# Two more token pairs transposed by way of DRAM, the key sum read as a row of G, and statistics and normalisation moved to ScalarE

## The chip, the core and the metric

The kernel runs on one core of a Trainium2 chip. The metric is the device time of one execution in microseconds (us). Five engines work side by side, each through its own queue in order: PE (TensorE, matrix products), DVE (VectorE), ACT (ScalarE), POOL (GpSimd) and SP (SyncE, which only issues transfers here). They wait for each other on semaphores. L12 is line 12 of the kernel.

## The reference, cut to what matters

Inputs are x of 2048 tokens by 512, weights wqkv (512 x 1536) and wo (512 x 512), and w_gate, w_up (512 x 1792) and w_down (1792 x 512).

```python
xn = (x - mean) / sqrt(var + 1e-5)                 # over the 512 columns
q, k, v = heads of xn @ wqkv                       # 32 heads of 16
phi(t) = where(t > 0, t + 1, exp(t)) + 1e-6
kv  = einsum("bhsd,bhse->bhde", phi(k), v)
z   = einsum("bhsd->bhd", phi(k))
num = einsum("bhqd,bhde->bhqe", phi(q), kv)
den = einsum("bhqd,bhd->bhq", phi(q), z)[..., None] + 1e-6
s   = (num / den) @ wo
g   = silu((gelu(xn @ w_gate) * (xn @ w_up)) @ w_down)
out = x + s * g
```

## The kernel before, in words

The 2048 tokens are 16 tiles of 128 rows. Two tiles make a pair, and there are 8 pairs (n = 0 to 7): pair 0 is tiles 0 and 4, pair 1 is 1 and 5, pair 2 is 2 and 6, pair 3 is 3 and 7, pairs 4 to 7 are (8, 12), (9, 13), (10, 14), (11, 15). Every float32 operand of a large product is split in a high and a low part (`split`: ACT makes the high part, DVE or POOL the low one), and a product is three passes of PE: high by high, high by low, low by high. Most large products are done by a scheme of 7 block products in place of 8 (X, Y and Z are its PSUM banks in the attention part; FX, FY, FZ and dX, dY, dZ in the feed-forward part).

The stages are these. First come the tokens, up to some 125 us: `ln` normalises a tile (statistics by two DVE instructions, the inverse root by POOL, xn by DVE), `transp` turns it, `split_x` and `forms` make the operands of the products, and q and k follow, with `phi` on ACT and DVE. `gacc` accumulates G = xn^T phi(k) in four banks (gps). Then kv = Wv^T G (pkv, L988) and M = kv wo (pm) are made once. Then the feed-forward part runs for the second half of the tokens (p = 1) and the first half (p = 0); between them the accumulators of p = 1 go through silu on ACT. Last come s = phi(q)/den M (sps) and the output.

Names that the change touches:

- `transp` (L621): for pairs below TX, PE turns the four 128 x 128 blocks of a tile (pt, L643) and ACT copies the bank. From TX on, xn is made by ACT (L565), written to DRAM (xn_d), read back in another layout (xq), and turned by one DVE instruction (`squares`, L617). TX is 6, so pairs 6 and 7 go by DRAM.
- `phi` (L705): for each tile two ACT instructions (relu of -v, exp) and one DVE instruction.
- `zacc` (L722): POOL adds phi(k) of each tile to an accumulator; at the end two PE passes (pz, L933) sum it over rows, and ACT copies it to zq. POOL multiplies phi(q) by zq for the denominators (L960).
- ACT holds one table of functions at a time: one for exp, one for gelu, one for silu. Each change issues an ACT_TABLE_LOAD.
- `warm` (L472): 12 products of a constant with itself ahead of the first real work on PE.

The order on every engine is not that of the code. The code makes a list of some 3,600 operations with their dependencies, and `ORDER` (L18) is a written-out permutation of that list: operation numbers in the order in which they are issued, each to its engine's queue. So each engine's queue is a subsequence of ORDER.

Of the kernel before, what the change touches and what calls it, by code (L numbers as in the profile page):

```python
# [14 lines left out]
P = 128  # L15
# [147 lines left out]
]  # L163

TABLES = {"exp": "exp", "gelu": "gelu", "silu": "silu"}
# [123 lines left out]
def pool(n):  # L289
    return 0.18 + 0.0021 * n  # L290
# [1168 lines left out]
```

## Time and profile before

| | |
|---|---|
| three runs | 566.92, 567.49, 567.54 us; median 567.49 |
| the profiled execution | 566.9 us in all, of which the span from first to last instruction is 564.8 us |
| PE busy | 557.8 us, 2630 matmul records |
| DVE busy | 493.2 us |
| ACT busy | 360.8 us |
| POOL busy | 253.1 us |
| transfers | 141.29 MB, mean 250 GB/s |

The time of the profiled execution lies 2.1 us above its span (566.9 less 564.8). "Busy" of PE counts pipelined products whose ends are modelled, so the distance between two starts tells more than a duration. In rows of the timeline the first column is the start in us from the span's start, the second how long the row's instructions took together, and the bracket at the end says how long the engine was idle ahead of it and what ended that.

### The profile page before, as it was taken

What the parts mean: (1) busy time and instruction counts of PE and PEld (TensorE: products, weight loads), DVE (VectorE), ACT (ScalarE), POOL (GpSimd) and SP (SyncE); (2) the same over time, 40 slices, a digit from 0 to 9 for tenths busy, and PEclk for the clock granted to TensorE, in tenths of its full rate; (3) what the DMA queues carried; (4) which work ended last, traced back from release to release, by engine and by line L of the source; (5) the groups of instructions that cost most, each with busy time, mean ns of one, the idle gap of its engine ahead of it and who ended that gap; (6) DMA issues with size and microseconds to landing.
All of it is one profiled execution on the core that took longest, in us unless ns stands there. A gap on an engine that the chain in (4) does not pass through costs nothing.

```text
span 564.8 us, 7902 instructions
## 1 busy us (share of the span) xinstructions
PE 557.8 (99%) x2630; PEld 487.0 (86%) x2630; DVE 493.2 (87%) x774; ACT 360.8 (64%) x668; POOL 253.1 (45%) x237
## 2 busy tenths in 40 slices
PE   8999999999999999999999999999999999999997
PEld 6888888888888888888888888888888888888886
DVE  7999999987798999999888776774889989898997
ACT  5987898877677876564536467867555636354730
POOL 4656677757786876431251940430413212314200
PEclk9999999999999999999999999999999999999999
DMA  7378967879978668158867998696757475778776
GB/s 266 104 217 273 274 203 233 255 223 322 352 241 300 240 234 339 43 201 311 265 233 216 389 339 335 239 344 254 243 187 242 173 247 194 233 228 286 239 247 239
DMA packets 78952, 141.29 MB, mean 250 GB/s; under 512 B 4672, under 2 KB 47680, under 8 KB 74944
## 3 DMA queue, kind: packets, MB, share of 16 engines
q1 hardware_dynamic: 78912, 140.79, 72.9%
q8 instruction: 21, 0.34, 0.2%
q14 instruction: 19, 0.16, 0.1%
HBM read 87.82 MB, written 52.95 MB: 249 GB/s over the span
## 4 chain that ended last, share of the span: by engine, by line
PE 91%; DVE 5%; DMA 2%; issue 1%; SPq 1%; ACT 0%; DVEq 0%; ACTq 0%
PE FX L442 26%; PE FZ L442 13%; PE dX L442 12%; PE gps L442 7%; PE FY L442 6%; PE dY L442 6%; PE X L442 6%; PE sps L442 4%; PE dZ L442 3%; PE Z L442 3%; PE q L442 2%; PE k L442 2%; PE Y L442 1%; DVE acc L1119 1%; PE pt L643 1%; DMA wk<-in_A_wqkv 1%
## 5 line engine op out<-in xcount | busy, mean ns | idle before, releaser
L442 PE MATMUL FX<-Xh,w 128*128 128x512 f32 x448 | 125.4, 379 | 0.0
L442 PEld LDWEIGHTS FX<-Xh,w 128*128 128x128 f32 x448 | 84.7, 189 | 12.0
L404 POOL TENSOR_TENSOR sums<-draw 128x256 f32<-128x256 f32 x28 | 26.5, 951 | 109.6 <-DVE dl L404 56.3
L1165 POOL TENSOR_TENSOR h<-h,g 128x512 f32<-128x512 f32 x28 | 39.5, 1411 | 65.9 <-DVE h L404 64.2
L442 PE MATMUL FX<-Xl,w 128*128 128x512 f32 x224 | 66.0, 379 | 0.0
L442 PE MATMUL FZ<-Xh,w 128*128 128x512 f32 x224 | 64.4, 379 | 0.0
L398 ACT COPY dY<-dX 128x512 f32<-128x512 f32 x56 | 32.1, 573 | 46.2 <-DVE acc L1119 28.4
L398 ACT COPY fu<-FX 128x512 f32<-128x512 f32 x56 | 32.7, 585 | 23.3 <-PE FX L442 19.4
L442 PEld LDWEIGHTS FX<-Xl,w 128*128 128x128 f32 x224 | 42.3, 189 | 6.0
L442 PEld LDWEIGHTS FZ<-Xh,w 128*128 128x128 f32 x224 | 42.3, 189 | 6.0
L398 ACT CAST hfh<-sums 128x512 fp32r<-128x512 f32 x56 | 34.5, 619 | 14.3 <-DVE sums L404 14.3
L442 PE MATMUL dX<-hfh,dh 128*128 128x512 f32 x112 | 41.9, 380 | 0.1
L442 PE MATMUL dX<-hfl,dh 128*128 128x512 f32 x112 | 41.5, 380 | 0.0
L442 PE MATMUL dX<-hfh,dl 128*128 128x512 f32 x112 | 41.0, 379 | 0.0
L1119 DVE TENSOR_TENSOR acc<-acc,dY 128x512 f32<-128x512 f32 x48 | 32.7, 681 | 8.9 <-PE dY L442 8.7
L404 DVE TENSOR_TENSOR hfl<-sums,hfh 128x512 fp32r<-128x512 f32 x56 | 40.2, 728 | 0.1
L404 POOL TENSOR_TENSOR tmp<-raw 128x256 f32<-128x256 f32 x28 | 29.1, 1049 | 20.1 <-DVE we L404 10.6
L1119 DVE TENSOR_TENSOR acc<-acc,dX 128x512 f32<-128x512 f32 x48 | 32.7, 683 | 5.5 <-PE dX L442 5.2
L960 POOL TENSOR_TENSOR qz<-qz,zq 128x512 f32<-128x512 f32 x16 | 23.3, 1456 | 23.1 <-DMA qz<-q_d 18.3
L442 PE MATMUL FY<-Xh,w 128*128 128x512 f32 x112 | 33.1, 379 | 0.0
L442 PE MATMUL FZ<-Xl,w 128*128 128x512 f32 x112 | 33.0, 379 | 0.0
L404 DVE TENSOR_TENSOR hfl<-h,hfh 128x512 fp32r<-128x512 f32 x42 | 32.2, 774 | 0.6 <-ACT hfh L398 0.6
(222 smaller groups left out, 1517.7 us busy)
## 6 DMA issues: line engine op xcount, KB each, us to landing
w<-w_d SPq DMA_DIRECT2D x17, 1792.0 KB, 7.9
w_d<-w SPq DMA_DIRECT2D x11, 1792.0 KB, 8.8
draw<-in_B_w_down SPq DMA_DIRECT2D x14, 512.0 KB, 4.0
w_d<-we SPq DMA_DIRECT2D x18, 256.0 KB, 2.2
x<-in_A_x SPq DMA_DIRECT2D x16, 256.0 KB, 3.3
q_d<-qp SPq DMA_DIRECT2D x16, 256.0 KB, 3.7
qz<-q_d SPq DMA_DIRECT2D x16, 256.0 KB, 3.1
q<-q_d SPq DMA_DIRECT2D x16, 256.0 KB, 3.8
```

What stands on the lines that cost most here:

```text
L398: do("ACT", act(n, src.psum), lambda o, i: nc.scalar.copy(o, i), dst, src, name=name)
L404: do(eng, c, lambda o, p, q: getattr(e, f"tensor_{op}")(o, p, q), dst, a, b, name=name)
L442: nc.tensor.matmul(o if r is None else o[:, r], a, turned(b), start=first, stop=made == self.passes[r], skip_group_check=self.on or r is n ...
L643: nc.tensor.transpose(o[:, k, :], a[:, j * P:(j + 1) * P], b)
L960: do("POOL", pool(D), lambda o, z: nc.gpsimd.tensor_mul(o, o, z.unsqueeze(1).to_broadcast([P, KT, P])), rows_of(q), zq, name="u")
L1119: do("DVE", dve(D), lambda o, i: nc.vector.tensor_add(o, o, i), o, ps, name="acc")
L1165: do("POOL", pool(NC), lambda o, i: nc.gpsimd.tensor_mul(o, o, i), h, g, name="h")
```

## The change

ORDER is written anew from end to end (3,622 operations), so all engines' queues differ. The code changes beside it are:

- TX goes from 6 to 4: pairs 4 and 5 go by DRAM too, and PE turns 8 tiles in place of 12.
- For tiles 2, 6, 3 and 7 (`XA`) xn is made by ACT, with a small DVE instruction for the bias (nb).
- For tile 4 (`SUMMED`), the second tile that is used, mean and variance come from two ACT instructions with an accumulated output (a copy and a square); DVE's two statistics instructions of it go.
- `added` adds 1 as well, so that `phi` on its results needs one ACT instruction (exp with a bias of -1) in place of two; this holds for 12 of the 32 calls.
- zacc and its 16 POOL additions, the two PE passes and the copies to zq go. In their place column 0 of each xn tile is set to 1 (16 small DVE instructions) ahead of its split, so that row 0 of G is the sum of phi(k). That row goes to DRAM and comes back spread over the partitions by four transfers. Because a row of xn sums to zero, subtracting the first row of Wv from all its rows makes up for the lost column (four subtractions, two by POOL and two by DVE).
- The warm-up products are 16 in place of 12.

```diff
 ORDER = [
-    988, 5, 0, 4, 7, 2, 10, 8, 11, 12, 9, 17, 6, 1, 18, 24, 16, 19, 20, 15, 28, 25, 13, 21, 29, 56, 62, 61, 63, 65, 116, 14, 57, 75, 117, 58, 118, 67,
...
-WARM = 12, 2
+WARM = 16,2
...
+    z_d = dram_view([1, D], "z_d")
...
-    zacc = const("zacc", [P, D])
-    do("POOL", 0.6, lambda o: nc.gpsimd.memset(o, NT * EPS), zacc)
...
-    TX = 6
+    TX = 4
...
+    XA = [(2, 6), (3, 7)]
+
+    SUMMED = [(4,)]
...
+        if ts in SUMMED:
...
+                for k, f in enumerate((AF.Copy, AF.Square)):
+                    do("ACT", 0.75, lambda o, a, x, b=None, f=f: nc.scalar.activation(o, x, f, accum_out=a, **({} if b is None else {"bias": b})),
+                       xns[t], mv[:, i, k:k + 1], xs[t], *([mv[:, i, 0:1]] if k else []), more=(mv,), name="sum")
...
+        if ts in XA:
+            nb = little("nb", f"nb{ts[0]}", [P, n])
...
+                do("ACT", 0.72, lambda o, i, r, b: nc.scalar.activation(o, i, AF.Identity, bias=b, scale=r),
+                   v, xs.pop(t).map(lambda ap: ap.rearrange("p (q g d) -> p q g d", q=KT, d=32)), rstd[:, i:i + 1], nb[:, i:i + 1], name=f"xn{t}")
...
+        do("DVE", 0.1, lambda o: nc.vector.memset(o, 1.0), (x[0] if isinstance(x, tuple) else x)[:, 0:1], name="one", port=False)
...
-        tt("DVE", "add", c, e, ps, D, name)
+        do("DVE", 0.6, lambda o, i, j: nc.vector.scalar_tensor_tensor(o, i, 1.0, j, op0=ALU.add, op1=ALU.add), c, ps, e, name=name)
...
+        if not v.psum:
+            do("ACT", act(D), lambda o, i, b: nc.scalar.activation(o, i, AF.Exp, bias=b), r, v, neg_one, name="exp")
+            p0 = U("p", range(24, 28), f"{nm}p{t}")
+            do("DVE", 0.6, lambda o, i, j: nc.vector.scalar_tensor_tensor(o, i, 1.0, j, op0=ALU.min, op1=ALU.max),
+               p0, r, v, name="phi")
+            return p0
...
-        do("POOL", pool(D), lambda o, i: nc.gpsimd.tensor_add(o, o, i), zacc, p0, name="zacc")
...
-    do("PE", 2 * PASS, run_z, pz, ones_r, *zs, key="z")
...
+    dma(z_d(0, slice(None)), GT[0][0:1], 2)
+    for k in range(KT):
+        dma(zq[32 * k:32 * k + 32].map(lambda ap: ap.rearrange("p (g d) -> p g d", d=32)),
+            z_d(0, slice(None)).map(lambda ap, k=k: ap.rearrange("o (g q d) -> o q g d", q=KT, d=32)[:, k].to_broadcast([32, KT, 32])), 16)
...
+    w0 = tile_in("up", 29, [P, D], F32, "w0")
+    dma(w0, ext(wqkv[0:1, 2 * D:3 * D].to_broadcast([P, D])), 256)
+    for c in range(KT):
+        tt("DVE" if c % 2 else "POOL", "sub", wv[c], wv[c], w0, D, "wv")
```

What the new ORDER makes of the queues is shown at three places. In the rows, x4 and xn4 are tile 4 and its normalised form, pt4 its bank of transposes, kq the split weights of q and k, k00 the first product bank (tile 0), Xh and Xl the split operands.

The first place is the start. PE's queue before:

```order
L472 MATMUL warm_100<-blk_93 128x128 x12
L643 MATMUL pt0_154<-blk_93,xn0_148 128x128 x4
L472 MATMUL warm_100<-blk_93 128x128 x2
L442 MATMUL k00_170<-kq0_135,Xh0_163 128x512
L442 MATMUL k00_170<-kq1_150,Xh0_163 128x512
L442 MATMUL k00_170<-kq0_135,Xh0_163 128x512 x3
L643 MATMUL pt4_196<-blk_93,xn4_189 128x128 x4
```

PE's queue there now:

```order
L473 MATMUL warm_101<-blk_94 128x128 x16
L680 MATMUL pt0_165<-blk_94,xn0_158 128x128 x2
L473 MATMUL warm_101<-blk_94 128x128 x2
L680 MATMUL pt0_165<-blk_94,xn0_158 128x128 x2
L443 MATMUL k00_193<-kq0_138,Xh0_182 128x512 x2
L680 MATMUL pt4_199<-blk_94,xn4_150 128x128 x4
```

Two products of k00 stand ahead of tile 4's transposes where five stood. DVE's queue at the same place before, from the variance of tile 0 on:

```order
L555 TENSOR_SCALAR ve0_139<-mv0_133 128x1
L573 TENSOR_SCALAR xn0_148<-x0_97,mv0_133,rstd0_141 128x4x4x32
L552 BN_STATS st4_152<-x4_121 128x6
L552 BN_STATS st1_165<-x1_123 128x6
L553 BN_AGGR mv4_168<-st4_152 128x2
L553 BN_AGGR mv1_172<-st1_165 128x2
L555 TENSOR_SCALAR ve4_174<-mv4_168 128x1
L552 BN_STATS st5_176<-x5_125 128x6
L553 BN_AGGR mv1_172<-st5_176 128x2
L555 TENSOR_SCALAR ve1_186<-mv1_172 128x2
L573 TENSOR_SCALAR xn4_189<-x4_121,mv4_168,rstd4_179 128x4x4x32
```

DVE's queue there now:

```order
L581 TENSOR_SCALAR ve0_144<-mv0_136 128x1
L566 TENSOR_SCALAR mv4_151<-mv4_151 128x1
L610 TENSOR_SCALAR xn0_158<-x0_98,mv0_136,rstd0_146 128x4x4x32
L578 BN_STATS st1_163<-x1_128 128x6
L563 TENSOR_SCALAR ve4_172<-mv4_151 128x1
L579 BN_AGGR mv1_174<-st1_163 128x2
L578 BN_STATS st5_176<-x5_130 128x6
L579 BN_AGGR mv1_174<-st5_176 128x2
L724 MEMSET xn0_158 128x1
L581 TENSOR_SCALAR ve1_187<-mv1_174 128x2
L571 TENSOR_SCALAR xn4_150<-x4_124,mv4_151,rstd4_180 128x4x4x32
```

A small instruction on tile 4's sum (L566) now stands ahead of xn0, and xn4 still stands behind the statistics of tiles 1 and 5. In SP's queue the load of x4 has moved from fourth to third place, ahead of the second piece of weights.

The second place is the switch between the two halves of the feed-forward part, on ACT. (FY, fu and dY are copies out of PSUM, g is gelu, acc1 under L1346 or L1380 is silu on the finished accumulators.) A piece of ACT's queue there before:

```order
L1079 ACT_TABLE_LOAD
L1079 ACTIVATE g22_14_3783<-g22_14_3783 128x512
L398 CAST hfh0_0_3826<-h11_15_3820 128x512
L1079 ACTIVATE g21_14_3831<-FX14_3612 128x512
L1346 ACT_TABLE_LOAD
L1346 ACTIVATE acc1_0_2134<-acc1_0_2134 128x512
L398 COPY fu3_15_3852<-FX15_3698 128x512
L1346 ACTIVATE acc1_1_2261<-acc1_1_2261 128x512
```

The tightest piece of it now:

```order
L399 COPY FY18_4078<-FX18_4054 128x512
L399 COPY dY00_0_4004<-dX00_0_3908 128x512
L1380 ACT_TABLE_LOAD
L1380 ACTIVATE acc1_1_2305<-acc1_1_2305 128x512
L1113 ACT_TABLE_LOAD
L1113 ACTIVATE g12_16_4032<-g12_16_4032 128x512
L399 COPY acc0_2_4119<-dY00_0_4004 128x512
L399 COPY fu2_18_4126<-FX18_4054 128x512
```

The silus are spread more thinly among the gelus: ACT's whole queue held 7 table loads before and holds 11 now, and all four new ones are at this switch (8 there in place of 4).

The third place is the end. The last rows of PE before (sps131 and sps130 are the two halves of the last tile, 256 columns each):

```order
L442 MATMUL sps130_5812<-pqh_5417,Ml_5157 128x256 x4
L442 MATMUL sps131_5800<-pqh_5417,Mh0_4075 128x256 x2
L442 MATMUL sps131_5800<-pqh_5417,Mh1_4270 128x256 x2
L442 MATMUL sps131_5800<-pqh_5417,Mh0_4075 128x256 x2
L442 MATMUL sps131_5800<-pqh_5417,Mh1_4270 128x256 x2
L442 MATMUL sps130_5812<-pqh_5417,Mh0_4075 128x256 x2
L442 MATMUL sps130_5812<-pqh_5417,Mh1_4270 128x256 x2
L442 MATMUL sps130_5812<-pqh_5417,Mh0_4075 128x256 x2
L442 MATMUL sps130_5812<-pqh_5417,Mh1_4270 128x256 x2
```

The last rows of PE now:

```order
L443 MATMUL sps131_5785<-pqh_5456,Ml_5152 128x256 x4
L443 MATMUL sps131_5785<-pqh_5456,Mh0_4406 128x256 x2
L443 MATMUL sps131_5785<-pqh_5456,Mh1_4330 128x256 x2
L443 MATMUL sps10_5808<-pqh_5456,Ml_5152 128x512 x4
L443 MATMUL sps10_5808<-pqh_5456,Mh0_4406 128x512 x2
L443 MATMUL sps10_5808<-pqh_5456,Mh1_4330 128x512 x2
L443 MATMUL sps10_5808<-pqh_5456,Mh0_4406 128x512 x2
L443 MATMUL sps10_5808<-pqh_5456,Mh1_4330 128x512 x2
```

The halves come earlier, and the last thing that PE makes is a whole tile of 512 columns (sps10); DVE's last two instructions and the last transfer have its size.

More of the change, by code (lines that the diff above doesn't have):

```diff
@@ L464 @@
     do("DVE", 0.1, lambda o: nc.vector.memset(o, -0.5), neg_half, port=False)
+    neg_one = tile_in("sm", "no", [P, 1], F32, "neg_one")
+    do("DVE", 0.1, lambda o: nc.vector.memset(o, -1.0), neg_one, port=False)
     do("POOL", 0.8, lambda o: make_identity(nc, o), ident)
-    zacc = const("zacc", [P, D])
-    do("POOL", 0.6, lambda o: nc.gpsimd.memset(o, NT * EPS), zacc)
     den_eps = tile_in("sm", "de", [P, H // KT], F32, "den_eps")
@@ L549, in ln @@
         mv = little("mv", f"mv{ts[0]}", [P, n, 2])
+        if ts in SUMMED:
+            ve = little("ve", f"ve{ts[0]}", [P, n])
+            rstd = little("rs", f"rstd{ts[0]}", [P, n])
+            for i, t in enumerate(ts):
+                xns[t] = U("xn", range(4, 9), f"xn{t}")
+                for k, f in enumerate((AF.Copy, AF.Square)):
+                    do("ACT", 0.75, lambda o, a, x, b=None, f=f: nc.scalar.activation(o, x, f, accum_out=a, **({} if b is None else {"bias": b})),
+                       xns[t], mv[:, i, k:k + 1], xs[t], *([mv[:, i, 0:1]] if k else []), more=(mv,), name="sum")
+                    if k:
+                        do("DVE", 0.1, lambda o, v: nc.vector.tensor_scalar(o, v, 1.0 / D, EPS_LN, op0=ALU.mult, op1=ALU.add),
+                           ve[:, i:i + 1], mv[:, i, 1:2], port=False)
+                    else:
+                        do("DVE", 0.1, lambda o, v: nc.vector.tensor_scalar_mul(o, v, -1.0 / D), mv[:, i, 0:1], mv[:, i, 0:1], port=False)
+            do("POOL", 0.2 + 0.36 * n, lambda o, i, j: nc.gpsimd.tensor_tensor(o, i, j.to_broadcast([P, n]), op=ALU.pow),
+               rstd, ve, neg_half)
+            for i, t in enumerate(ts):
+                v = xns[t].map(lambda ap: ap.rearrange("p (g q d) -> p q g d", g=KT, d=32))
+                do("DVE", 0.46, lambda o, i, m, r: nc.vector.tensor_scalar(o, i, m, r, op0=ALU.add, op1=ALU.mult),
+                   v, xs.pop(t).map(lambda ap: ap.rearrange("p (q g d) -> p q g d", q=KT, d=32)),
+                   mv[:, i, 0:1], rstd[:, i:i + 1], name=f"xn{t}")
+                xns[t] = xns[t], v
+            return
         for i, t in enumerate(ts):
@@ L569, in ln @@
             return
+        if ts in XA:
+            nb = little("nb", f"nb{ts[0]}", [P, n])
+            do("DVE", 0.11, lambda o, i, r: nc.vector.scalar_tensor_tensor(o, i, -1.0, r, op0=ALU.mult, op1=ALU.mult),
+               nb, mv[:, :, 0], rstd)
         for i, t in enumerate(ts):
+            if ts in XA:
+                xns[t] = U("xn", range(4, 9), f"xn{t}")
+                v = xns[t].map(lambda ap: ap.rearrange("p (g q d) -> p q g d", g=KT, d=32))
+                do("ACT", 0.72, lambda o, i, r, b: nc.scalar.activation(o, i, AF.Identity, bias=b, scale=r),
+                   v, xs.pop(t).map(lambda ap: ap.rearrange("p (q g d) -> p q g d", q=KT, d=32)), rstd[:, i:i + 1], nb[:, i:i + 1], name=f"xn{t}")
+                xns[t] = xns[t], v
+                continue
             xns[t] = U("xn", range(4, 9), f"xn{t}")
@@ L922 @@
         GT.append(g)
-    pz = bank(7, "pz")
-    ones_r = tile_in("sm", "onr", [P, P], F32R, "ones_r")
-    do("ACT", 0.2, lambda o, i: nc.scalar.copy(o, i), ones_r, ones, name="ones")
-    zs = [tile_in("up", n, [P, D], F32R, f"z{n}") for n in (29, 32)]
-    split(*zs, zacc, D, "z")
-    def run_z(o, a, *zs):
-        for n, z in enumerate(zs):
-            nc.tensor.matmul(o, a, turned(z), start=n == 0, stop=n == 1)
-    do("PE", 2 * PASS, run_z, pz, ones_r, *zs, key="z")
-    zq = const("zq", [P, P])
-    def turn_z(o, i):
-        for k in range(KT):
-            rows = slice(32 * k, 32 * k + 32)
-            nc.scalar.copy(o[rows].rearrange("p (g d) -> p g d", d=32),
-                           i[rows].rearrange("p (g q d) -> p g q d", q=KT, d=32)[:, :, k])
-    do("ACT", 0.7, turn_z, zq, pz, name="zb")
+    zq = const("zq", [P, P])
+    dma(z_d(0, slice(None)), GT[0][0:1], 2)
+    for k in range(KT):
+        dma(zq[32 * k:32 * k + 32].map(lambda ap: ap.rearrange("p (g d) -> p g d", d=32)),
+            z_d(0, slice(None)).map(lambda ap, k=k: ap.rearrange("o (g q d) -> o q g d", q=KT, d=32)[:, k].to_broadcast([32, KT, 32])), 16)
     do("DVE", 0.2, lambda o, i: nc.vector.tensor_reduce(o, i, axis=AX.X, op=ALU.add), den_eps,
@@ L1379 @@
     g_take(100)
-    pe_keys += keys[2:5] + ["z"] + keys[5:KV] + [("kv", g) for g in range(KT)] + keys[KV:KV + 3]
+    pe_keys += keys[2:KV] + [("kv", g) for g in range(KT)] + keys[KV:KV + 3]
     pe_keys += [("m", g) for g in range(KT)] + keys[KV + 3:]
```

287 rows, old and new, of the table ORDER are left out of this document.

## The prediction

> **What bounds the kernel now.** I read the page first, then what PE waited for, then PE's busy time by stretch.
>
> ```profile
> span 564.8 us, 7902 instructions
> PE 557.8 (99%) x2630; PEld 487.0 (86%) x2630; DVE 493.2 (87%) x774; ACT 360.8 (64%) x668; POOL 253.1 (45%) x237
> PE 91%; DVE 5%; DMA 2%; issue 1%; SPq 1%; ACT 0%; DVEq 0%; ACTq 0%
> ```
>
> ```profile
> PE pt L643 <- DVE xn L573: 1.2, 1, 1.2
> PE warm L472 <- DVE blk L462: 1.1, 1, 1.1
> PE k L442 <- ACT kq L398: 0.3, 1, 0.3
> ```
>
> ```profile
> 12.00:120.00 108.00, 107.97 (x518) 93.85 (x517) 103.57 (x173) 93.05 (x175) 71.64 (x65) 1.00 0.73 221
> 340.00:365.00 25.00, 25.00 (x117) 21.89 (x117) 16.48 (x25) 19.15 (x31) 7.03 (x7) 1.00 0.72 268
> 560.00:565.00 5.00, 0.86 (x8) 0.67 (x6) 1.70 (x5) 0.00 (x0) 0.00 (x0) 0.89 0.38 134
> ```
>
> PE is busy 99% of the span, carries 91% of the chain that ended last, and its listed waits are all in the start. (In the stretches the columns after the length are PE, PEld, DVE, ACT, POOL.) So three things make the time: when PE's unbroken run begins, how many passes stand in it, and what follows its last pass. DVE at 103.57 of 108 us in the token stage is full too, yet PE waits for nothing there.
>
> **The passes.** What one costs is read from the starts, since busy times overlap.
>
> ```profile
> 41.66 1.03 PE L442 MATMUL X<-kq,Xh 128*128 128x512 f32 x4
> 42.52 0.59 PE L442 MATMUL X<-kq,Xl 128*128 128x512 f32 x2
> 45.54 0.60 PE L643 MATMUL pt<-blk,xn 128*128 128x128 f32 x4
> 45.90 0.46 PE L442 MATMUL gps<-pkh,xnl 128*128 128x512 f32 x1
> 46.20 0.59 PE L442 MATMUL gps<-pkh,xnh 128*128 128x512 f32 x2
> ```
>
> Four passes of 512 columns take 42.52 - 41.66 = 0.86 us, 0.215 each. A tile's four transposes take 45.90 - 45.54 = 0.36, and the pass behind them 0.30 in place of 0.215: 0.445 for a tile. The change removes four tiles' transposes, 4 x 0.445 = 1.78 us, and the two z passes, 2 x 0.215 = 0.43. All lie inside the unbroken run, so 2.21 us come off, if what replaces them is on time.
>
> **What replaces them.** For the four tiles DVE turns in place of PE, ACT makes xn in place of DVE, and each tile goes to DRAM and back.
>
> ```profile
> L617 DVE STREAM_TRANSPOSE xt<-xq 128x512 f32<-128x512 f32 x4 | 4.3, 1119 | 0.0
> L573 DVE TENSOR_SCALAR xn<-x,mv,rstd 128x512 f32<-128x512 f32 x12 | 8.0, 669 | 0.7 <-POOL rstd L557 0.7
> L565 ACT ACTIVATE xn<-x,nb,rstd 128x512 f32<-128x512 f32 x4 | 3.0, 806 | 0.0
> L709 ACT ACTIVATE kr<-kr 128x512 f32<-128x512 f32 x16 | 10.1, 631 | 0.2
> L722 POOL TENSOR_TENSOR zacc<-zacc,kp 128x512 f32<-128x512 f32 x16 | 24.0, 1499 | 6.5 <-DVE kp L711 6.2 <-DVE mv L553 0.2
> xn_d<-xn SPq DMA_DIRECT2D x4, 256.0 KB, 3.1
> xq<-xn_d SPq DMA_DIRECT2D x4, 256.0 KB, 3.0
> ```
>
> DVE gains 4 x 1.12 = 4.5 us of turning, 16 small writes and four nb, and loses 8 x 0.67 = 5.4 of xn and tile 4's statistics; two subtractions replace the z split. That is nearly even. ACT gains 8 x 0.81 = 6.4 and the two sums, and loses 12 x 0.63 = 7.6 of the first phi step and four copies from PSUM. POOL loses 24 us and gains two subtractions. So no engine of the token stage is fuller, and I cost this at nothing. Its cover is distance in the queues: a tile's way to DRAM and back is 3.1 + 3.0 us, and on DVE's queue 18 rows now stand between pair 4's nb and its first turning, where pair 6 had 14 before without a wait. SP issues eight more 256 KB transfers, and the loads queued behind each xq wait with it. If that cover is gone, the first product of pair 4 waits on PE, and the z-bound transfers (two in a row) can hold POOL's first qz and the weight sums behind it; POOL is idle for 55% of the span, so I cost that at nothing too.
>
> **The start.**
>
> ```profile
> 3.42 0.69 DVE L552 BATCH_NORM_STATS2 st<-x 128x6 f32<-128x512 f32 x1 [2.36 <-DMA x<-in_A_x]
> 5.12 2.68 POOL L404 TENSOR_TENSOR kq<-wk,kq 128x512 fp32r<-128x512 f32 x2
> 5.19 1.48 DVE L573 TENSOR_SCALAR xn<-x,mv,rstd 128x512 f32<-128x512 f32 x1 [0.68 <-POOL rstd L557]
> 5.42 0.62 ACT L398 CAST kq<-wk 128x512 fp32r<-128x512 f32 x1 [0.58 <-DMA wk<-in_A_wqkv]
> 7.42 0.65 ACT L398 CAST Xh<-pt 128x256 fp32r<-128x256 f32 x2 [1.39 <-PE pt L643]
> 8.27 0.68 DVE L552 BATCH_NORM_STATS2 st<-x 128x6 f32<-128x512 f32 x1
> 9.88 0.66 PE L643 MATMUL pt<-blk,xn 128*128 128x128 f32 x4
> ```
>
> The third transfer lands at 5.4 (the cast at 5.42 waited for it). It is now x4: ACT's sum ends near 6.1, and DVE's small step on it, which stands ahead of xn0, releases xn0 near 6.25 in place of 5.19. But xn0 took 1.48 us before, beside POOL's first kq, against a mean of 0.67 over the twelve; so it ends near 6.7 as before. ACT then has a cast and the square ahead of Xh, which comes near 7.3 to 7.5, as before. The warm-up's four extra products fill PE's wait.
>
> In the Trainium skill, SBUF — State Buffer, section "SBUF: two separate sides", the port pair that DVE and GpSimd share is an exclusive lock held for a whole instruction. By that rule xn0 ends just behind POOL's kq whether it is asked at 5.2 or at 6.25; the 1.48 us agree with it.
>
> Then xn4. It still stands behind the statistics of tile 5, the sixth load in both orders, which began at 8.27 before. If that goes at 8.0 (its load, no longer behind other DVE work), xn4 ends near 9.7 and tile 4's transposes start at 9.7 to 9.9, as before (9.88). Ahead of them, PE now does two products of k00, where five stood. From there on I find no wait in either queue, so three passes have moved into the unbroken run: 3 x 0.215 = 0.65, less up to 0.2 for the earlier xn4. I take +0.5; ends -0.3 (statistics of tile 4 off DVE let all of it start earlier) and +1.2 (a wait for tiles 1 and 5 comes on top).
>
> **The end.**
>
> ```profile
> 558.69 0.68 DVE L1335 TENSOR_TENSOR acc<-acc,sps 128x512 f32<-128x512 f32 x1
> 559.40 0.69 DVE L404 TENSOR_TENSOR acc<-acc,sxr 128x512 f32<-128x512 f32 x1
> 560.90 0.42 DVE L1333 TENSOR_TENSOR acc<-acc,sps 128x256 f32<-128x256 f32 x1
> 561.35 0.42 DVE L404 TENSOR_TENSOR acc<-acc,sxr 128x256 f32<-128x256 f32 x1
> out_yT<-acc SPq DMA_DIRECT2D x1, 256.0 KB, 2.5
> out_yT<-acc SPq DMA_DIRECT2D x1, 128.0 KB, 1.9
> ```
>
> After the last pass come a product, an addition and a store. On 256 columns that was 560.90 to 561.77, 0.87 us, and 1.9 for the store. On 512 columns it is 558.69 to 560.09, 1.40, and 2.5: 0.53 + 0.6 = 1.1 us more. Ends 0.7 (the store is not longer) and 1.4 (DVE, full here, is late by 0.3).
>
> **The switch between the halves.** Four more table loads on ACT.
>
> ```profile
> 342.46 0.57 ACT L398 COPY dY<-dX 128x512 f32<-128x512 f32 x1 [1.39 <-DVE acc L1119]
> 343.05 1.28 ACT L1346 ACT_TABLE_LOAD   x1
> 344.34 0.63 ACT L1346 ACTIVATE acc<-acc 128x512 f32<-128x512 f32 x1
> ```
>
> A change of table took 1.31 us, from the copy's end at 343.03 to 344.34. Four more are 5.2 us. ACT was busy 19.15 of the 25 us from 340 to 365, so 5.85 were idle, with four loads in it. The work fits, and the new queue spreads it beyond those 25 us; in its tightest piece two loads and two functions (2 x 1.31 + 2 x 0.63 = 3.9 us) stand ahead of a copy (fu) for which PE has other passes meanwhile. I take 0; ends 0 and +2.6 (two loads uncovered).
>
> ScalarE: Activation LUTs in the Trainium skill, section "What ACT_TABLE_LOAD costs", states 1283 ns for the load and 1380 ns for a drain, 2.66 us a switch. The trace agrees on the first and shows no second part. By the page, four more would be 10.6 us, beyond the idle time; that is the last rival below.
>
> **The sum.** -1.78 - 0.43 + 0.5 + 1.1 = -0.6 us. The profiled execution took 566.9 (span 564.8 and 2.1 around it), so 566.3. It is the lowest of the three runs, 0.6 under their median of 567.49; I keep its frame. No change can be told within 0.2%, 1.1 us.
>
> **The rivals.**
>
> *The start costs nothing, and the end less.* With the start at -0.3, the end at +0.7 and the passes at -2.21 it is -1.8: 565.1. For it speaks that DVE, full from 10 us on, is relieved of tile 4's statistics (0.69 and more) at its busiest place, and POOL's 24 us beside it go; against it, the order of rows at the start as told. It becomes faster than can be told once start and end together cost less than 1.1.
>
> *The table loads reach PE.* Place: the last piece of ACT's queue quoted ahead. If the copy FY18 comes over 2 us late there, PE waits at the next FX product, and two loads show: +2.6, in sum +2.0, 568.9: slower. It decides from 1.7 us of uncovered wait on. For it: ACT's idle time and the new loads are nearly equal (5.85 and 5.2). Against: four loads in 20 us before caused no listed wait.
>
> *Pair 4 or 5 is late on its way through DRAM.* A longer transfer ahead of an xq makes it late:
>
> ```profile
> xh_d<-Xh SPq DMA_DIRECT2D x4, 896.0 KB, 4.9
> ```
>
> 4.9 - 3.0 = 1.9 us for each pair, 3.8 for both, in sum +3.2: 570.1. Against it: pairs 6 and 7 went this way with no idle time ahead of their turning.
>
> *Each switch of table costs twice the load.* Then 10.6 less 5.85 idle is 4.8 uncovered, in sum +4.2: 571.1. Against it are the rows of 342.46 to 344.34.
>
> **How the numbers follow.** The sum: 0.45 (own range 565.8 to 568.0). Start and end cheaper: 0.34. Table loads: 0.10; DRAM way: 0.08; double switch: 0.03. So faster 0.34, same 0.45, slower 0.21. The range goes from 0.6 below the cheap case to 0.3 above the table loads and leaves out the two dearest cases (0.11) and the edges of the others: 564.5 to 569.2.
>
> **What would show it.** PE should have 32 transposes and no pz row; tile 4's transposes should start at 9.7 to 9.9 with two k products ahead; from the last pass to the span's end there should be 5.0 us in place of 3.9 (560.90 to 564.8); the chain should show no ACT at the switch. It is wrong if PE's list of waits names an xt, an Xh of pairs 4 and 5, or fu, or if tile 4's transposes start more than 0.5 us off.

## The result: slower by 3.7 us, and the profile after

| | before | after |
|---|---|---|
| median (20 runs each) | 567.51 us | 571.20 us |
| lowest and highest | 566.84 to 568.39 | 567.41 to 573.87 |
| profiled execution, and its span | 566.9, 564.8 | 570.45, 568.6 |

The ratio is 1.0066, with a 95% interval of 1.0053 to 1.0078. The forecast was 566.3, the range 564.5 to 569.2; the median lies above it. The spread from run to run has grown from 1.6 us to 6.5. All times and ratios here are of executions at the full clock; one execution each of the runs loads and den1 below ran at a lowered clock (0.948 and 0.656) and is left out.

The page of the changed kernel, its first lines and the chain that ended last:

```profile
span 568.6 us, 7932 instructions
PE 558.8 (98%) x2620; PEld 485.9 (85%) x2620; DVE 493.1 (87%) x791; ACT 361.6 (64%) x662; POOL 215.3 (38%) x222
PE 81%; DVE 8%; DMA 5%; ACT 2%; POOL 1%; issue 1%; SPq 0%; DVEq 0%; POOLq 0%; ACTq 0%
```

No engine is busy for over 1 us more (PE 558.8 us after 557.8, DVE 493.1 after 493.2, ACT 361.6 after 360.8, POOL 215.3 after 253.1), but PE carries 81% of the chain where it carried 91%, and DVE and transfers carry 13% where they carried 7%. What PE waited for (us in total, times, longest):

```profile
PE dY L443 <- ACT dY L399: 1.7, 1, 1.7
PE warm L473 <- DVE blk L463: 1.1, 1, 1.1
PE k L443 <- ACT Xh L399: 0.7, 1, 0.7
PE pm L443 <- DVE kv L405: 0.6, 1, 0.6
PE q L443 <- DVE a L405: 0.4, 1, 0.4
PE FZ L443 <- DVE g L405: 0.4, 1, 0.4
PE pt L680 <- DVE xn L610: 0.3, 1, 0.3
```

Four new waits stand in the middle of the run: q at 26 us, pm at 156, FZ at 279, dY at 325. Behind DVE stand transfers. DVE's own waits on them, without that for the first x (2.4 us before, 2.3 after), before and then after (on POOL's qz it waits for a load of qz one step further back):

```profile
DVE rall L962 <- POOL qz L960: 3.8, 3, 1.6
DVE q L1226 <- DMA q<-q_d: 1.3, 1, 1.3
```

```profile
DVE q L1260 <- DMA q<-q_d: 5.1, 4, 2.4
DVE rall L992 <- POOL qz L990: 5.0, 4, 2.6
DVE wvo L405 <- DMA w<-in_A_wqkv: 1.8, 1, 1.8
DVE xt L654 <- DMA xq<-xn_d: 1.7, 2, 0.9
```

These are 13.6 us where there were 5.1.

All starts of PE in both traces give an account of the 3.8 us between the spans. A distance between starts up to 0.31 us counts as a pass, what is over a pass's 0.216 in a longer one as a stall:

| | forecast | measured |
|---|---|---|
| passes removed | -2.21 | -2.2 |
| start, up to 12 us | +0.5 | +0.9 |
| stalls behind 12 us | 0 | +4.4 (1.2 before, 5.6 after) |
| from the last pass to the end | +1.1 | +0.7 |
| sum | -0.6 | +3.8 |

Of the 5.6 us of stalls 1.0 stands at 26 to 29 us, 0.8 at 156, 1.2 at 273 to 283 and 2.0 at 323 to 326; the rest are single distances 0.1 too long.

A second account takes the same pass, counted from the end, in before and in three profiles of the changed kernel (after, and the runs "again" and "again2" below), and says by how much the changed kernel is later:

| place in before | after | again | again2 |
|---|---|---|---|
| 108 us | -0.4 | -0.2 | -0.8 |
| 256 us | +0.3 | +0.5 | +1.2 |
| 343 us | +3.2 | +3.5 | +2.5 |
| 537 us | +3.2 | +3.5 | +2.5 |

In after and again 2.9 and 3.0 us of the loss arise between 256 and 343 us, where the second group of denominators is made. In again2 it is 1.3 there, and 2.0 between 108 and 256. From 343 to 537 nothing is added in any of them.

### The profile page after: what moved, and what is told of

Same layout as the page of the kernel before. It is cut to its first block, busy times and chain, and to the rows that moved or that the text cites. A ratio compares the mean times of both kernels' runs of the same rounds, so it can differ in the third digit from the quotient of the medians.

```text
span 568.6 us, 7932 instructions
## 1 busy us (share of the span) xinstructions
PE 558.8 (98%) x2620; PEld 485.9 (85%) x2620; DVE 493.1 (87%) x791; ACT 361.6 (64%) x662; POOL 215.3 (38%) x222
## 4 chain that ended last, share of the span: by engine, by line
PE 81%; DVE 8%; DMA 5%; ACT 2%; POOL 1%; issue 1%; SPq 0%; DVEq 0%; POOLq 0%; ACTq 0%
PE FX L443 22%; PE dX L443 11%; PE FZ L443 10%; PE gps L443 7%; PE sps L443 6%; PE dY L443 6%; PE X L443 6%; PE FY L443 5%; PE dZ L443 3%; PE Z L443 3%; DMA qz<-q_d 2%; DMA t_d<-sums 2%; PE q L443 2%; PE Y L443 1%; DVE acc L1153 1%
## 5 line engine op out<-in xcount | busy, mean ns | idle before, releaser
L405 POOL TENSOR_TENSOR sums<-draw 128x256 f32<-128x256 f32 x28 | 23.5, 840 | 141.1 <-DMA draw<-in_B_w_down 95.0
L1199 POOL TENSOR_TENSOR h<-h,g 128x512 f32<-128x512 f32 x28 | 38.3, 1371 | 41.3 <-DVE h L405 35.7
L405 POOL TENSOR_TENSOR tmp<-raw 128x256 f32<-128x256 f32 x28 | 27.6, 995 | 53.0 <-DVE we L405 23.9
L405 DVE TENSOR_TENSOR hfl<-sums,hfh 128x512 fp32r<-128x512 f32 x56 | 41.7, 747 | 0.8 <-ACT hfh L399 0.6
L399 ACT CAST hfh<-h 128x512 fp32r<-128x512 f32 x42 | 25.8, 618 | 9.3 <-PE dY L443 4.4
```

The costliest lines, as they stand in the source:

```text
L399: do("ACT", act(n, src.psum), lambda o, i: nc.scalar.copy(o, i), dst, src, name=name)
L405: do(eng, c, lambda o, p, q: getattr(e, f"tensor_{op}")(o, p, q), dst, a, b, name=name)
L1199: do("POOL", pool(NC), lambda o, i: nc.gpsimd.tensor_mul(o, o, i), h, g, name="h")
```

## The experiments

Each run's ratio is to the kernel before, run beside it on the same chip. Most edits only move operations. MOVES is a list of pairs (operation, the one behind which it is put) that is applied to ORDER in turn:

```diff
-        return [self.ops[n] for n in ORDER]
+        order = list(ORDER)
+        for n, behind in MOVES:
+            order.remove(n)
+            order.insert(order.index(behind) + 1, n)
+        return [self.ops[n] for n in order]
```

### Three executions of one kernel: again

No edit.

> The changed kernel, unaltered, for a second profile and as the measure of the runs beside it. Theory (the new order queues DVE's and ACT's work behind transfers that land late): ratio 1.005 to 1.008, some 3 to 5 us more than before, spread over several us from run to run, and in the second profile TensorE's long waits stand at other places, or at the same places with other lengths, according to which qz, t_d or w transfer was late; the 1.74 us on dY at 325 is not there if that qz load took 3.5 us and not 5.5. Rival (four more table loads): the same waits at the same places in both profiles, beside the ACT_TABLE_LOAD records.

570.48 us, ratio 1.0055 (1.0035 to 1.0075). The stalls stand at the same places with other lengths: at 324 it is 1.12 us and not 1.90, at 274 it is 0.66 and not 0.17. Here is the chain behind the wait on dY in the profile of after (start, us, what):

```profile
315.25 0.70 DVE rall L992
...
315.96 5.54 DMA qz<-q_d
...
321.63 1.27 POOL qz L990
...
322.93 0.69 DVE rall L992
323.61 0.61 DVE sums L405
...
324.77 0.59 ACT dY L399
...
325.40 0.48 PE dY L443
```

phi(q) of a tile is loaded into qz, POOL multiplies it, DVE reduces it to the denominators, and only then is the one buffer free for the next load. Nobody needs these denominators soon. But DVE takes its queue in order: `sums`, on which ACT's copies and then PE depend, stands behind the reduction, which stands behind the load. How long did this one load take in the three profiles of the unaltered changed kernel (the last figure, us from issue to landing)? After:

```profile
qz<-q_d SPq DMA_DIRECT2D x1, 256.0 KB, 5.5
```

Again:

```profile
qz<-q_d SPq DMA_DIRECT2D x1, 256.0 KB, 4.8
```

Again2:

```profile
qz<-q_d SPq DMA_DIRECT2D x1, 256.0 KB, 3.8
```

PE's stall behind it is 1.90, 1.12 and 0.15 us. The landing differs by 1.7 us, the stall by 1.75. So in these three profiles one transfer's luck goes through to PE one for one. In profiles of edited kernels that keep this load in its place the relation is looser: 4.2 us of landing went with a stall of 0.98 in dve2, 3.5 with 0.72 in start2, 5.3 with 1.59 in tail. This is one of the places that make the runs differ, but not the only one: the spans of the three profiles (568.6, 568.9 and 567.9 us) lie closer together than their stalls here.

### The denominators drawn apart: spread

```diff
+MOVES = [
+    (2363, 2228), (2362, 2223), (2361, 2119), (2360, 2117), (2359, 2116), (2358, 2290),
...
```

> Only the seven last denominators of the second group are moved: their loads of qz stand 7.4 us apart in the order and not 5 to 8.6, with 5 us and more between a load and POOL's product. The arithmetic is unaltered. Theory: the 1.9 us stall of TensorE at 323 goes and part of the other waits after 300 with it; 1.5 to 2.5 us faster than the changed kernel, ratio to before 1.002 to 1.005, less spread from run to run. Rival (the start and the end alone make the difference): no change, ratio 1.005 to 1.008.

580.03 us, ratio 1.0224 (1.0204 to 1.0244): against the expectation, 9 us slower. The stall at 324 has shrunk to 0.2, but a load now fell at a worse place. From its chain:

```profile
332.88 8.67 DMA s_d<-so
...
341.62 8.14 DMA qz<-q_d
...
349.89 1.27 POOL qz L1002
...
351.19 0.69 DVE rall L1004
351.87 1.80 DVE acc L1165 x3
```

```profile
345.00:349.00 4.00, 0.77 (x4) 0.34 (x2) 0.00 (x0) 0.00 (x0) 0.00 (x0) 0.98 1.01 406
349.00:353.00 4.00, 0.00 (x0) 0.00 (x0) 1.81 (x4) 0.45 (x1) 1.94 (x2) 0.50 0.03 11
353.00:357.00 4.00, 3.28 (x8) 2.66 (x9) 1.86 (x4) 1.70 (x3) 0.00 (x0) 0.50 0.98 331
```

The rows of the second fence are busy time by stretch (PE, PEld, DVE, ACT, POOL, then granted clock, DMA share, GB/s). While the load of 256 KB was under way for 8.14 us, the DMA engines were wholly busy (1.01) with other transfers, and every compute engine came to a stop. Even distances in the order did not help here; the chain names what lies behind the load and what moves beside it. The wait also halved PE's clock, to 0.50. In the Trainium skill, TensorE: Matmul & The Clock Gate, section "HAM oscillation — how this bites in real kernels", a wait on a transfer that outlasts the gate's window of some 3.4 us lets the next products start at half rate. The trace agrees: behind 8.1 us of waiting the clock was 0.50, behind 1.90 us in the changed kernel it stayed at 1.00. But 3.4 us is no safe bound by these runs: in den1b below a stall of 3.2 us was enough (0.57).

### A second buffer: two

```diff
+MOVES = [(2344, 2341), (2347, 2343), (2352, 2346), (2355, 2349), (2358, 2354), (2361, 2357)]
...
-        q = U("qz", [35], f"qz{t}")
+        s = spare(1)
+        q = s.part(s.res[8:9], (slice(None), 6)) if p == 0 and t % 2 else U("qz", [35], f"qz{t}")
...
-    spare(0)
     behind(0,
```

> The eight denominators of the second group get a second buffer (the row of the sums tile that only the turns use), every other one; their loads are issued right behind the reduction of the denominator two before, and POOL's product and DVE's reduction stay where they were in the changed kernel's queues. So 8 to 20 us of order lie between a load and its use, not 3 to 11. The arithmetic is unaltered. Theory (DVE's queue stands behind a reduction whose 256 KB load is late, since one buffer leaves it a few us): the stall on dY at 323 to 325 (1.1 to 1.9 us in four profiles of this order) is gone, no wait of DVE on POOL's qz over 0.5 us after 300; 1.0 to 2.0 us faster than the changed kernel of the earlier job, ratio to before 1.002 to 1.004. Rival (what is late there is DVE itself, or the table loads, and the load only stands ahead of it): the stall stays, ratio 1.005 to 1.007.

570.39 us, ratio 1.0046 (1.0031 to 1.0060). The wait on dY is gone from PE's list, and DVE waits on POOL's qz 1.6 us in place of 5.0:

```profile
PE dX L452 <- DVE acc L1163: 0.7, 2, 0.4
PE FZ L452 <- DVE g L414: 0.7, 1, 0.7
PE pm L452 <- DVE kv L414: 0.5, 1, 0.5
PE q L452 <- DVE a L414: 0.4, 1, 0.4
```

```profile
DVE rall L1002 <- POOL qz L1000: 1.6, 2, 1.2
```

0.21 us of that stall is left here, and 0.1 or nothing in the profiles of the five later runs with the second buffer (combo, best0, best, best1, best0b), where it is 0.15 to 1.90 in the profiles without one. So the cause of that stall is shown. But the gain, below 1 us, is less than the stall: 0.44 us came back at 329, where dX waits for DVE, and the stalls behind 12 us sum to 6.8 in this profile, not to less than 5.6.

### The start: start, start2, start3

```diff
+MOVES = [(57, 21), (58, 66), (59, 58), (60, 59), (82, 77)]
```

> Only the first microseconds are reordered: xn of token tile 0 ahead of the mean of token tile 4 on DVE, both casts of Xh ahead of the square of tile 4 on ACT, one k product more ahead of tile 4's transposes on TensorE. The arithmetic is unaltered. Theory: first transposes at 6.8 to 7.2 and not 7.73, first k product at 8.0 to 8.4 and not 9.57, at most 1 us gained of the time of the changed kernel (0.4 to 1.0): ratio to before 1.004 to 1.006. Rival (the start carries the whole loss): ratio at or below 1.000. Rival (the start's loss is taken up later, since what stands behind it waits for transfers anyway): no change.

573.80 us, ratio 1.0100 (1.0084 to 1.0117): slower. The product put ahead was ready (start2's expectation below has that otherwise); the square of tile 4, now behind the casts, made xn4 late, and PE stood 1.47 us before tile 4's transposes.

```diff
-WARM = 16,2
+WARM = 12,2
+MOVES = [(57, 21), (63, 21), (64, 63), (66, 68), (68, 66), (58, 68), (59, 58), (60, 59)]
```

> The start alone, without the extra k product that waited for a weight cast in the earlier try: xn of tile 0 ahead of the step on tile 4's sum on DVE, both casts of Xh ahead of tile 4's square on ACT in the order of their transposes, the two transpose groups of tile 0 in the order of before, 12 warm-up products and not 16. The arithmetic is unaltered. Theory: warm-up over by 5.5 to 6.5 and not 6.4 to 7.9, first transposes at 6.7 to 7.2, first k product within 1.3 us behind them (1.84 in the changed kernel), so at 8.0 to 8.5 and not 8.9 to 9.7; 0.5 to 1.2 us faster than the changed kernel, ratio to before 1.004 to 1.005. Rival (tile 4's xn is the later one then, and gives it back): less than 0.3 us.

573.39 us, ratio 1.0105 (1.0090 to 1.0120). The first k product comes at 8.13 as expected, but PE then waits 1.96 us for tile 4: the rival holds, and more than holds.

```diff
-WARM = 16,2
+WARM = 14,2
+MOVES = [(58, 57), (28, 58), (59, 21), (60, 59), (61, 117), (91, 63)]
```

> The start alone, third try: tile 4's square ahead of the cast of the second weight piece on ACT (which waits for a later load), its variance and xn right behind xn of tile 0 on DVE, its transposes ahead of the first k products on TensorE, 14 warm-up products. The arithmetic is unaltered. Theory (two k products, not five, stand ahead of tile 4's transposes, and those wait for xn of tile 4; the earlier tries made that one later): transposes of tile 4 at 8.3 to 9.6 and not 9.7 to 10.3, no wait over 0.5 us after the first k product, 0.5 to 0.9 us faster than the changed kernel: ratio to before 1.003 to 1.0055. Rival (what stands later in the order gives it back): no gain, 1.0055 to 1.007.

572.36 us, ratio 1.0090 (1.0071 to 1.0109). xn4 did start at 8.51, but beside POOL's kq:

```profile
8.51 1.48 DVE L580 TENSOR_SCALAR xn<-x,mv,rstd 128x512 f32<-128x512 f32 x1
10.13 0.63 PE L689 MATMUL pt<-blk,xn 128*128 128x128 f32 x4 [1.74 <-DVE mv L588]
```

So it took 1.48 us in place of 0.55 and the transposes came no earlier, now with nothing ahead of them. Three tries, three misses: of the orders tried, the changed kernel's own start is the best.

### The end: tail

```diff
+MOVES = [
+    (3592, 3599), (3590, 3592), (3591, 3590), (3617, 3591), (3619, 3617), (3618, 3619),
...
```

> Only the last microseconds are reordered: the full tile of the last eight passes ahead of the two half tiles, so that a 256-column product, its addition and a 128 KB store end the kernel. The arithmetic is unaltered. Theory: from the end of TensorE's last pass to the end of the span 4.2 us and not 4.9, 0.5 to 0.9 us gained of the time of the changed kernel: ratio to before 1.004 to 1.006. Rival (the store's landing sets the end whatever its size): less than 0.3 us gained.

570.85 us, ratio 1.0061 (1.0048 to 1.0073), beside 570.48: no gain that can be told. In its profile the stretch from PE's last start to the end is 4.4 us and not 4.9, which the spread of the rest covers.

### Two instructions of DVE: dve2

```diff
+MOVES = [(400, 33), (1005, 1004)]
```

> Two single instructions of DVE are moved in the changed kernel's order: the statistics of the third pair behind the low parts of a (token stage), and the low part of kv ahead of a low part of w that waits for POOL (behind a load of qz). The arithmetic is unaltered. Theory: the stall of 0.57 us at 26 (in all five profiles of this order) and that of 0.4 to 1.0 us at 156 are gone; 0.8 to 1.2 us faster than the changed kernel, ratio to before 1.004 to 1.005. Rival (the moved instruction makes another wait): less than 0.4 us gained, a new wait of TensorE on DVE within 10 us of the old place.

570.74 us, ratio 1.0049 (1.0036 to 1.0063). The stalls at 26 and 156 are gone (0.14 left at 26.7). PE, earlier by 0.5 us, then waits 0.43 at 65, 0.56 at 174 and 0.97 at 328 where after had none. The first two are not proof of the rival, since they also stand in profiles without this edit (0.43 at 65 in tail, 0.59 at 174 in again2). So the theory holds for the two stalls, and the gain stays unproven.

### Combinations: combo, best0, best

combo is two, start2, dve2 and tail, with the four turns drawn apart; best0 is two, dve2 and tail with the turns further apart; best is best0 with start3.

```diff
+MOVES = [
+    (1075, 1757), (1076, 1075), (1078, 1076), (1077, 1078), (2003, 2001), (1079, 2013),
+    (1080, 1079), (1082, 1080), (1081, 1082), (1083, 1885), (1084, 1083), (2338, 1084),
...
```

> All of it together: the second buffer, the start, the two moved instructions, the half tiles at the end, and the four turns of the first group drawn apart by 2 to 4 us (their reads and writes of DRAM go through one buffer; stalls of 0.6 to 1.1 us at 273 to 281). The arithmetic is unaltered. Theory: the stalls of the changed kernel add up to 7.0 us; with 2 left as in the kernel before, and 0.5 us less at the end, 564.5 to 566.0 us, ratio 0.995 to 0.9975, and a spread from run to run under 2.5 us. Rival (transfers that are late move the wait elsewhere, whatever is reordered): ratio 0.999 or more.

> Second buffer, the two moved instructions of DVE, the half tiles at the end, and the first group's turns drawn further apart (the second behind the product h that held ACT in the try before); the start is that of the changed kernel. The arithmetic is unaltered. Theory: of the changed kernel's stalls those at 26, 156, 274 to 280 and 324 are gone, some 3 us, and 0.5 at the end: 567.0 to 568.5 us, ratio 0.999 to 1.002. Rival (transfers that are late move the wait elsewhere): ratio 1.003 to 1.006, with new waits of TensorE on DVE behind an xq, q or qz.

> The same with the start of the third try. The arithmetic is unaltered. Theory: 0.5 to 0.9 us below the run beside it, ratio to before 0.998 to 1.0005. Rival: a stall near 105 to 110, as in the earlier combination, since pair 4's or 5's xq is late for a DVE that is earlier; no gain over the run beside it.

combo 572.26 (1.0064 to 1.0090), best0 570.15 (1.0031 to 1.0057), best 573.75 (1.0094 to 1.0121). In the two with an altered start PE stands 1.8 to 2.0 us ahead of tile 4's transposes, and again at 105 to 112. In combo it first waits 1.18 us behind DVE, which waits for an xq, and then 0.67 behind ACT, which waits for a write of weights (w_d<-we) to free its buffer:

```profile
105.47 1.08 DVE L672 STREAM_TRANSPOSE xt<-xq 128x512 f32<-128x512 f32 x1 [3.19 <-DMA xq<-xn_d]
106.83 0.62 ACT L417 CAST we<-raw 128x512 fp32r<-128x512 f32 x1 [2.55 <-DMA w_d<-we]
```

In after the longest wait of DVE for an xq was 0.9, and ACT's wait at this place 0.40. In best only the second of the two stands there (0.81 us of stall behind 1.37 of waiting).

In the profile of best0 the stalls at 26, 156, 274, 280 and 324 are 0.15 or less, as intended. But its stalls behind 12 us still sum to 5.9 us: others stand in their place, the longest (0.72) at 295. By the ratio the rival holds.

### Fewer table loads: loads

```diff
+MOVES = [(2308, 2312), (2320, 2308), (2316, 2600), (2317, 2316), (2322, 2316), (2318, 2322), (2319, 2318), (2314, 2318)]
```

> Only the eight silus on the finished accumulators are regrouped on ACT, four and four, so that the switch between the halves has 4 table loads as before the change and not 8; the queues of PE, DVE and POOL stay. The arithmetic is unaltered. Theory (the loads lie in idle time of ACT; TensorE waits behind transfers instead): the same time as the changed kernel, ratio to before 1.005 to 1.007. Rival (table loads reach TensorE): 1.3 to 5.2 us gained, ratio 0.996 to 1.003.

573.72 us, ratio 1.0107 (1.0092 to 1.0122). Four loads fewer did not help, the kernel got slower by some 3 us; neither theory had that, and where the 3 us arise stays open. That the loads cost nothing in the changed kernel rests on the second table above: no lag is added between 343 and 537 us.

### What holds the pace: pool, den1, best1

```diff
+        eng, e = ("POOL", nc.gpsimd) if t in (8, 9, 12, 13, 10) else ("DVE", nc.vector)
-        do("DVE", dve(D), lambda o, a, b: nc.vector.tensor_sub(
+        do(eng, dve(D), lambda o, a, b: e.tensor_sub(
```

> Five of the sixteen subtractions xnl (tiles 8, 9, 12, 13, 10) are made by POOL and not by DVE, at the same places of the order: 5 x 0.68 = 3.4 us less for DVE between 50 and 80 us, 5 x 1.3 us more for POOL, which is idle there. The arithmetic is unaltered. If DVE's amount of work holds the pace: the stall at 65 (0.43) and those at 26 to 66 in sum fall, 0.4 to 1.0 us faster than the changed kernel, ratio 1.004 to 1.005. If transfers hold it: DVE waits for xq as much longer, no change, 1.0055 to 1.007.

573.05 us, ratio 1.0097 (1.0066 to 1.0127): slower. At 65 only 0.1 us is left, but that was so in again2 without any edit. And 2.3 us of new stalls stand at 105 to 113. DVE waits 2.2 us there for an xq, which costs PE 0.2, and 0.66 stands behind ACT, which waits 1.56 for w_d<-we as in combo. The other 1.46 stand behind DVE itself, whose instructions take 1.50 and 1.61 us beside POOL's new subtractions and 0.68 in after:

```profile
108.90 1.27 POOL L737 TENSOR_TENSOR xnl<-xn,xnh 128x512 fp32r<-128x512 f32 x1
109.22 1.50 DVE L413 TENSOR_TENSOR Xl<-xt,Xh 128x512 fp32r<-128x512 f32 x1
```

So this run does not answer its question: what it takes off DVE it gives back in part, by slowing DVE.

```diff
+MOVES = [
+    (1046, 1309), (1052, 1205), (1051, 1283), (1050, 1285), (1049, 1169), (1048, 1277),
...
```

> In the first group the product of the second denominator moves behind the weight sums that stood behind it on POOL, its reduction, the next two denominators and their loads with it (by 2 to 4 us); nothing else. The arithmetic is unaltered. If the qz load at the head of POOL's queue holds the pace near 155 to 160: the stall at 156 (0.4 to 1.0 us) is gone, and what follows at 160 to 176 stays under 0.3; 0.4 to 0.9 us faster than the changed kernel, ratio 1.004 to 1.005. If DVE's work does: the stall stays or comes back within 20 us, 1.0055 to 1.007.

> Second buffer, the two moved instructions, the turns drawn apart, the half tiles at the end, and both moves of the runs beside it. The arithmetic is unaltered. If both causes are met: 0.8 to 1.5 us faster than the combination without them (570.15), 568.6 to 569.4, ratio 1.002 to 1.0035. If the waits only move on: 570.0 or more, ratio 1.0044 or more.

den1 574.35 (1.0084 to 1.0144), best1, which is best0 with this move and pool's edit, 576.11 (1.0126 to 1.0177). den1 and the combination best0 were then run again, side by side with the unaltered kernel.

### Side by side: again2, best0b, den1b

Unaltered, best0 and den1 once more.

> The changed kernel, unaltered, as the measure for the two beside it on the same chip. Ratio 1.005 to 1.008; if this order of work is sensitive to the chip as well, the median lies over 572.

> The combination (second buffer, two moved instructions, turns drawn apart, half tiles at the end) once more. Theory (the waits are real losses and each one taken away counts in part): 0.8 to 1.8 us below the changed kernel beside it. Rival (what is taken away comes back in full): within 0.5 us of it.

> The second denominator's product behind the weight sums on POOL, alone. If the qz load at the head of POOL's queue holds the pace at 156: its stall gone, 0.4 to 0.9 us below the changed kernel beside it. If the order behind it suffers more (later denominators, loads of weights behind them on SP): as slow as or slower than the changed kernel, with stalls between 160 and 230 that its profile lacks.

again2 570.44 (ratio 1.0054, 1.0037 to 1.0070), best0b 568.81 (1.0021, 1.0007 to 1.0034), den1b 574.58 (1.0124, 1.0104 to 1.0144). So the combination gains 1.6 us on the changed kernel; the first time it was 0.6, by the ratios of best0 and again (1.0044 and 1.0055). 0.5 of it is the end (4.4 us from PE's last start in place of 4.9); the stalls in best0b's profile still sum to 5.7 us. It is still slower than the kernel before, and so is every version tried. den1 is slower by its order, and den1b's profile, of the same kernel, says why in four rows:

```profile
154.21 6.92 DMA qz<-q_d
...
161.26 1.27 POOL qz L1000
...
163.16 0.69 DVE h L415
...
163.89 1.18 PE FX L453 x3
```

One load was moved by 4 us to a place where it takes 6.92 us; DVE's h, which PE needs, stands behind its reduction, and PE stalls 3.2 us, then runs at a clock of 0.57 for four more.

## Why the prediction was wrong, step by step

**The passes** came out: -2.2 us.

**The start** was sized at +0.5 and measured +0.9, within its ends. Tile 4's transposes start at 10.27 in this profile (9.98 and 9.91 in the two others), somewhat behind the 9.7 to 9.9 forecast, with two k products ahead, as forecast. The small step on tile 4's sum did hold up xn0, longer than thought, since x4 landed at 6.3 and not at 5.4:

```profile
6.32 0.63 ACT L560 ACTIVATE xn<-x 128x512 f32<-128x512 f32 x1 [1.64 <-DMA x<-in_A_x]
7.07 0.15 DVE L566 TENSOR_SCALAR mv<-mv 128x1 f32<-128x1 f32 x1 [2.56 <-ACT xn L560]
7.14 0.54 DVE L610 TENSOR_SCALAR xn<-x,mv,rstd 128x512 f32<-128x512 f32 x1
9.57 0.70 PE L443 MATMUL k<-kq,Xh 128*128 128x512 f32 x2 [0.74 <-ACT Xh L399]
```

"From there on I find no wait in either queue" was wrong at 26 us: 0.57 in every profile of this order, gone in dve2, so it is DVE's order. With what follows it up to 29 us it makes 1.0 us of the stalls.

**The end** was put at +1.1 and measured +0.7. DVE's two rows cost the 0.5 forecast:

```profile
564.08 0.69 DVE L1369 TENSOR_TENSOR acc<-acc,sps 128x512 f32<-128x512 f32 x1 [0.25 <-PE sps L443]
564.80 0.69 DVE L405 TENSOR_TENSOR acc<-acc,sxr 128x512 f32<-128x512 f32 x1
```

From their end at 565.49 to 568.6 are 3.1 us; before it was 564.8 - 561.77 = 3.0. So the store of twice the size cost 0.1 and not the 0.6 taken from the medians of the two sizes.

**The table loads** cost nothing, as forecast.

**The step that failed** is "I cost this at nothing. Its cover is distance in the queues", together with "POOL's first qz ... I cost that at nothing too". The term was 0 and measured +4.4 us, of which some 1.0 is DVE's order at 26 and the rest mostly waits for transfers. The working asked whether an engine has more to do, found none, and looked at distances for the parts that the diff names (xq of pairs 4 and 5). But ORDER (3,626 operations before and 3,628 now; 3,622 above is a slip) is new from end to end, and the stalls lie at parts that the diff doesn't name: the denominators (324), the turns (274 and 280), kv (156). The loads of denominators and of turns go through one buffer each, so a late one cannot be caught up by an earlier issue, and behind the instruction of DVE that waits stands one that PE needs. At 156 DVE's kv stands behind a sum that waits for POOL, which had waited 1.6 us for a qz. That is close to what the prediction named and cost at nothing, the weight sums behind a qz; POOL being idle for half the span was no cover, since there it waits for the load itself. Of the signs of being wrong that the prediction listed none came; it listed none for the denominators, the turns or kv.

The rival of a late xq named a mechanism of this kind at another place: in after DVE's waits there are 1.7 us and no stall is over 0.1, but in combo 1.18 us of stall stand behind such a wait.

The single stalls are explained, each by its chain and by a run in which it is gone. Not shown is that the loss can be had back: where those five stalls were taken away, in the profiled executions of best0 and best0b (570.5 us each), the stalls behind 12 us still sum to 5.9 and 5.7 us, no less than in after.

What may have made the transfers later is how busy the DMA engines are (the last figures but one), before and then after:

```profile
60.00:130.00 70.00, 69.97 (x332) 60.80 (x331) 64.03 (x104) 59.29 (x112) 48.22 (x44) 1.00 0.79 240
300.00:345.00 45.00, 44.86 (x208) 38.63 (x208) 35.35 (x55) 24.55 (x44) 21.33 (x17) 1.00 0.89 331
```

```profile
60.00:130.00 70.00, 70.00 (x326) 61.27 (x326) 63.27 (x113) 56.13 (x103) 28.19 (x34) 1.00 0.93 275
300.00:345.00 45.00, 43.27 (x201) 37.41 (x200) 36.26 (x55) 23.33 (x44) 22.46 (x20) 1.00 0.91 334
```

From 60 to 130 us the DMA engines are busy 0.93 of the time where it was 0.79. But from 300 to 345, where 1.5 us of after's loss arises, the share is nearly the same. That traffic is the cause there is argued, not shown: a kernel that moves less data wasn't tried. Nor is it settled why the kernel before bears its own waits so well: DVE waited there 3.8 us for qz too, with PE's stalls behind 12 us at 1.2. What stands behind each reduction differs, and in den1b and spread it was this that let one late load stop PE; a count for the whole of both orders wasn't made.

## What to carry to other kernels

When an order is written anew, go through every step of an in-order engine that waits for a transfer, not only those of the edit, and ask what stands behind it and when that is needed; take the longest landing in the trace for it, not the median (qz before: 3.1 us in the median and 6.0 at most; 5.5 to 8.1 where it hurt). The landing alone does not tell: the last load of qz took 10.8 us in after, and PE did not stall behind it. An engine that stands idle is no cover if it is idle on the same transfer. A spread from run to run that grows fourfold may be a sign of such waits: here one load's landing set one stall, microsecond for microsecond in three profiles. That such waits make up the whole spread is not shown; best0b, without that stall, still spread over 3.0 us.

## What the runs showed of the hardware that was not expected

A 256 KB load between the same two places took 3.8, 4.8 and 5.5 us in three executions of one kernel, and 6.92 and 8.14 where it was moved to; the last such load took 10.8, 10.7 and 10.4 us in the same three executions. An instruction of DVE on 128x512 took 1.50 us beside a subtraction on POOL (run pool) and 0.68 without it. A wait of 1.8 to 2.0 us at the very start was followed by passes of 0.43 us in start2, start3 and best (granted clock 0.74 from 10.1 to 13.8 us in start3), but not in combo with 2.03; in the changed kernel a stall of 1.90 at 323 left the clock at 1.00.
